# Retention unit by unit with 64-row matmuls, plain float32 scores and two PSUM banks

## The chip, the cores and the metric

One core of a Trainium2 chip runs the kernel. The metric is the device time of one execution in microseconds (us). Before the change the median of three runs is 960.05 us (959.32 to 961.3).

## The reference, cut to what matters

Three layers follow each other: a retention layer (linear attention with a decay per head) on 4 batches, 8 heads, 768 positions and head size 64; a feed-forward layer with an ELU on its 3072 tokens of 512 values; and a second one whose hidden 1024 values go through softmax-times-self and a layer norm.

```python
for t in range(S):
    state = gamma[None, :, None, None] * state + np.einsum('bhd,bhe->bhde', k[:, :, t], v[:, :, t])
    y[:, :, t] = scale * np.einsum('bhd,bhde->bhe', q[:, :, t], state)
...
x = np.ascontiguousarray(attn_out.transpose(0, 2, 1, 3)).reshape(B * S, H * D)
h = x @ w_in
g = np.where(h > 0.0, h, alpha * (np.exp(np.minimum(h, 0.0)) - 1.0))
return (g @ w_out).astype(np.float32)
```

## The kernel before, in words

**The retention.** Positions go in chunks of 128. A unit is four heads (two pairs) of one chunk; there are 48 units. For a pair the kernel needs: the scores k x q of each head, times a decay mask (line 187, or lines 201 to 203); the values, that is state x q (line 217) plus v x masked scores (line 219); the chunk's own k x v (line 223); the scaled result into `xf` (line 228); and the new state (lines 233 and 236). `xf` holds one block of 512 tokens.

The two heads of a pair share the 128 partitions, 64 each. Before the change the state is kept as a block diagonal 128 x 128 matrix per pair, so that one matmul serves both heads. The scores are made in two ways. For units 0 to 9 `kblk` holds k in a block diagonal with zeros and one plain float32 matmul per head runs over all 128 rows (line 186). For later units q and k are split into a high and a low part of the short float32 format (`split_unit`, on ScalarE and GpSimd), and one matmul of 256 columns per head gives two partial sums (line 199), which ScalarE and VectorE add up (lines 201 and 202).

**The feed-forward layers.** Every product of two float32 matrices is three matmuls of high and low parts (`mm3`, lines 65 to 67). Layer one runs over 6 blocks of 512 tokens, each in 16 steps s; a step makes one slice of the hidden layer (12 matmuls into `hp`, 128x512), its ELU, and 12 matmuls into the four `acc` banks, for the slice of two steps earlier. In block 0 the weights are prepared as well (`prep_w`: bits put together, clamped and split in high and low on VectorE, ScalarE and GpSimd). Layer two (from about 660 us) does 24 tiles of 128 tokens.

**The order.** The program's order is written out by hand, and every engine works its instructions off in that order; the SP queue issues all loads. First a prologue does units 0 to 7, which is the whole of block 0. Then each step does the matmuls into `hp`, then one pair of retention for the next block, then the matmuls into `acc`: pairs 18 to 95 lie in steps 0 to 77, one in each, and step 0 has pairs 16 and 17 as well. At a block's last step (k = 15) `xf` is split for the next block (`split_xh` on ScalarE, line 245, and `split_xl` on VectorE, line 250).

**PSUM.** `sc_bank` takes scores and `yu_bank` takes values and k x v; in the prologue three banks of each kind are used in turn, the others lent by `acc`.

## Time and profile before

| | |
|---|---|
| median of three runs | 960.05 us |
| the profiled execution | 957.76 us |
| its span, first to last instruction | 955.9 us |
| PE, matmuls busy | 928.9 us, 97% |
| VectorE (DVE) busy | 494.7 us, 52% |
| ScalarE (ACT) busy | 347.4 us, 36% |
| GpSimd (POOL) busy | 341.5 us, 36% |

The span is the time between the first and the last instruction of the profiled execution; 1.86 us of that execution lie around it. PE is the TensorE's matmuls, PEld its weight loads, which overlap them. Busy shares are means over stages with different limits: the stretch up to about 36 us is the prologue, that up to about 160 us is block 0 with its weight preparation, and the rest runs with prepared weights. Matmuls are pipelined, so that what a matmul costs is read from the start of one to the start of the next and not from its own length.

### The profile page before, as it was taken

The numbers are of one execution on the slowest core, as the hardware profiler recorded it, in microseconds if no ns is written. First come the engines' busy times: TensorE is split into PE (matmuls) and PEld (weight loads), VectorE is DVE, ScalarE is ACT, GpSimd is POOL, SyncE is SP. The second block draws the span as 40 slices with busy tenths as digits, with TensorE's granted clock in tenths as the row PEclk, the third lists the DMA queues.
The fourth block names the chain that finished last, engine by engine and source line by source line (L and its number), as shares of the span: only waits on it lengthen the run. The fifth ranks groups of instructions, "written<-read, shape, count | busy, mean of one in ns | idle before, by whom it ended". The sixth has DMA issues, their size and how long they took to land.

```text
span 955.9 us, 12630 instructions
## 1 busy us (share of the span) xinstructions
PE 928.9 (97%) x4776; PEld 760.0 (80%) x4776; DVE 494.7 (52%) x973; ACT 347.4 (36%) x629; POOL 341.5 (36%) x343
## 2 busy tenths in 40 slices
PE   6899999999999999999999999999999999999998
PEld 5677777888788887878788887888788888888886
DVE  3899997333443345333534328898633333333332
ACT  1355554333333334333332324443333333333332
POOL 2333232444534444444443423444322222222220
PEclk9999999999999999999999999999999999999999
DMA  8655551421142212322232214330211111111101
GB/s 253 195 177 179 182 171 39 121 78 53 64 121 78 77 48 78 113 78 77 70 91 77 80 67 138 95 91 20 77 45 45 45 45 44 45 45 45 45 23 44
DMA packets 43836, 82.67 MB, mean 86 GB/s; under 512 B 4096, under 2 KB 21120, under 8 KB 43776
## 3 DMA queue, kind: packets, MB, share of 16 engines
q1 hardware_dynamic: 43776, 81.88, 27.3%
q8 instruction: 37, 0.61, 0.3%
q14 instruction: 23, 0.19, 0.1%
HBM read 69.28 MB, written 12.58 MB: 86 GB/s over the span
## 4 chain that ended last, share of the span: by engine, by line
PE 79%; DVE 13%; DMA 2%; issue 2%; ACT 2%; SPq 1%; POOL 0%; ACTq 0%; DVEq 0%
PE hp L66 11%; PE hp L67 11%; PE hp L65 11%; PE acc L66 7%; PE acc L67 7%; PE acc L65 7%; PE op L66 5%; PE op L65 5%; PE op L67 5%; PE sc_bank L199 3%; PE yu_bank L219 2%; DVE wt L107 2%; PE tp L374 2%; DVE wt L108 2%; DVE xl L250 1%
## 5 line engine op out<-in xcount | busy, mean ns | idle before, releaser
L290 POOL TENSOR_TENSOR gl<-e,gh 128x512 fp32r<-128x512 f32 x80 | 108.1, 1351 | 249.2 <-ACT gh L282 201.7
L67 PE MATMUL acc<-gh,w1ol 128*128 128x512 f32 x384 | 150.7, 392 | 3.5 <-DVE w1ol L125 3.5
L67 PE MATMUL hp<-xh,w1il 128*128 128x512 f32 x384 | 150.4, 392 | 1.2 <-DVE w1il L125 1.2
L65 PE MATMUL acc<-gh,w1oh 128*128 128x512 f32 x384 | 151.2, 394 | 0.0
L66 PE MATMUL hp<-xl,w1ih 128*128 128x512 f32 x384 | 149.8, 390 | 1.1 <-DVE xl L250 0.9
L65 PE MATMUL hp<-xh,w1ih 128*128 128x512 f32 x384 | 149.9, 390 | 0.7 <-ACT xh L245 0.7
L66 PE MATMUL acc<-gl,w1oh 128*128 128x512 f32 x384 | 150.0, 391 | 0.0
L282 ACT CAST gh<-e 128x512 fp32r<-128x512 f32 x96 | 59.7, 622 | 199.7 <-DVE e L281 148.5
L271 ACT ACTIVATE e<-hp 128x512 f32<-128x512 f32 x80 | 47.8, 598 | 148.2 <-PE hp L67 147.3
L67 PEld LDWEIGHTS acc<-gh,w1ol 128*128 128x128 f32 x384 | 72.1, 188 | 21.2 <-DVE w1ol L125 6.3
L202 DVE TENSOR_TENSOR pt<-sa,sc_bank 128x256 f32<-128x256 f32 x60 | 25.3, 421 | 122.8 <-ACT sa L201 121.9
L67 PEld LDWEIGHTS hp<-xh,w1il 128*128 128x128 f32 x384 | 72.1, 188 | 18.9 <-DVE w1il L125 4.4
L66 PEld LDWEIGHTS hp<-xl,w1ih 128*128 128x128 f32 x384 | 72.1, 188 | 17.4 <-DVE xl L250 1.9
L65 PEld LDWEIGHTS hp<-xh,w1ih 128*128 128x128 f32 x384 | 72.1, 188 | 15.8 <-ACT xh L245 1.1
L65 PEld LDWEIGHTS acc<-gh,w1oh 128*128 128x128 f32 x384 | 72.2, 188 | 13.3 <-issue 0.5
L66 PEld LDWEIGHTS acc<-gl,w1oh 128*128 128x128 f32 x384 | 72.1, 188 | 12.8
L65 PE MATMUL op<-w2oh,zh 128*128 128x512 f32 x192 | 76.7, 399 | 0.0
L228 DVE TENSOR_TENSOR xf<-yu_bank,od_sb 128x256 f32<-128x256 f32 x43 | 18.1, 421 | 110.0 <-PE yu_bank L223 88.1
L66 PE MATMUL op<-w2ol,zh 128*128 128x512 f32 x192 | 74.8, 390 | 0.0
L67 PE MATMUL op<-w2oh,zl 128*128 128x512 f32 x192 | 74.8, 390 | 0.0
L67 PE MATMUL hp<-w2ih,yl 128*128 128x512 f32 x192 | 74.8, 389 | 0.0
L65 PE MATMUL hp<-w2ih,yh 128*128 128x512 f32 x192 | 74.8, 389 | 0.0
(101 smaller groups left out, 1573.1 us busy)
## 6 DMA issues: line engine op xcount, KB each, us to landing
in<-in_qkv SPq DMA_DIRECT2D x48, 384.0 KB, 4.4
qk<-in_qk_dup SPq DMA_DIRECT2D x30, 512.0 KB, 3.6
raw<-in_w_in SPq DMA_DIRECT2D x24, 512.0 KB, 4.3
raw<-in_w_out SPq DMA_DIRECT2D x24, 512.0 KB, 3.7
y_dr<-yt SPq DMA_DIRECT2D x24, 256.0 KB, 3.2
yin<-y_dr SPq DMA_DIRECT2D x24, 256.0 KB, 2.8
out<-ot SPq DMA_DIRECT2D x24, 256.0 KB, 2.0
kblk<-in_k_t SPq DMA_DIRECT2D x36, 64.0 KB, 4.5
```

The source lines that it names most:

```text
L65: nc.tensor.matmul(o, lh, rh, start=first, stop=False)
L66: nc.tensor.matmul(o, lh, rl, start=False, stop=False)
L67: nc.tensor.matmul(o, ll, rh, start=False, stop=last)
L107: nc.vector.scalar_tensor_tensor(b, t[:, :, 1], 0xC0000000, b, ALU.bitwise_and, ALU.bitwise_or)
L108: nc.vector.scalar_tensor_tensor(b, t[:, :, 0], 29, b, ALU.logical_shift_right, ALU.bitwise_or)
L199: nc.tensor.matmul(sc[:, j].rearrange("p a t -> p (a t)"), k2[:, 2 * i + j, :], q2[:, 2 * i + j].rearrange("p a t -> p (a t)"), start=True ...
L202: nc.vector.tensor_tensor(pt, sa, sc[:, :, 0, :], ALU.add)
L219: nc.tensor.matmul(yu[j * D:(j + 1) * D, i, 0, :], v[:, j * D:(j + 1) * D], pt[:, j, :], start=(c == 0), stop=True)
L271: nc.scalar.activation(e, h_t[s], AF.Exp)
L282: nc.scalar.copy(gh, e)
L290: engine.tensor_tensor(gl, e, gh.bitcast(F32), ALU.subtract)
L374: nc.tensor.transpose(tp[:, m, :], z[:, n, m * P:(m + 1) * P], ident)
```

## The change

The retention goes by units instead of pairs, and its tiles of the array change shape. `att_scores` multiplies k and q of one head on 64 rows (one half of the partitions), in plain float32 and with no zeros; heads j = 0 and j = 1 of a pair use the two row halves and write two banks. The state is no longer a block diagonal: it is 128 x 64 per pair, and `att_values` multiplies it in quarters, with row half j and column half i xor j, so that the four heads of a unit use the four quarters of the array. Rows of `xf` are permuted by that, and the host permutes the rows of the first weight matrix to match. Everything of a unit (values, k x v, scores) lies in the two banks of `ab`. `kblk`, `k_t`, `qk_dup`, `split_unit` and the sum of partial scores are gone; q, both forms of k, and v come in one load per unit, of the same bytes as before in units 0 to 9. The state's decay is read from a small table (`gm_sb`), so that one instruction serves both halves. In the steps a whole unit is done in each odd step, and none in the even ones, but for step 0.

```diff
--- before.py
+++ after.py
...
+    dm_sb = const.tile([P, 2, 2, 2 * P], F32, name="dm_sb")
     od_sb = const.tile([P, NP, P], F32, name="od_sb")
...
-        yu_bank = psa.tile([P, 512], F32, name="yu_bank")
+        ab = psa.tile([P, 2, 512], F32, name="ab")
         wb_p = ph1.enter_context(tc.tile_pool(name="wb", bufs=32))
...
@@ -145,95 +142,68 @@
         order2 = [("w2i", j) for j in range(2 * KD)] + [("w2o", j) for j in range(NF2)]
-        qk_t, in_t, hl_t, p_t = {}, {}, {}, {}
+        in_t, p_t = {}, {}
         def load_unit(u):
-            t = at_p.tile([P, 768], F32, tag="in", name="in", bufs=4)
+            t = at_p.tile([P, 4, 2 * P], F32, tag="in", name="in", bufs=4)
             nc.sync.dma_start(out=t, in_=qkv[u])
             in_t[u] = t
-            if u < UN:
-                for j in range(2):
-                    nc.sync.dma_start(out=kblk[u % 2][j * D:(j + 1) * D, :, j, :], in_=k_t[u, j * D:(j + 1) * D])
-        def load_qk(u):
-            t = hl_p.tile([P, 2, 4, P], F32, tag="qk", name="qk", bufs=1)
-            nc.sync.dma_start(out=t, in_=qk_dup[u - UN])
-            qk_t[u] = t
         def scale_k(u):
-            kt = in_t[u][:, 256:512].rearrange("p (h d) -> p h d", h=4)
+            kt = in_t[u][:, 2].rearrange("p (h d) -> p h d", h=4)
             h = 4 * (u % 2)
             nc.gpsimd.tensor_tensor(kt, kt, kd_sb[:, h:h + 4].unsqueeze(2).to_broadcast([P, 4, D]), ALU.mult)
-        def split_unit(u):
-            t = qk_t.pop(u)
-            q2 = hl_p.tile([P, 4, 2, P], F32R, tag="q2", name="q2")
-            k2 = hl_p.tile([P, 4, P], F32R, tag="k2", name="k2")
-            nc.scalar.copy(k2, t[:, 1])
-            nc.scalar.copy(q2[:, :, 0, :], t[:, 0])
-            nc.gpsimd.tensor_tensor(k2[D:], t[D:, 1], k2.bitcast(F32)[D:], ALU.subtract)
-            nc.gpsimd.tensor_tensor(q2[:, :, 1, :], t[:, 0], q2.bitcast(F32)[:, :, 0, :], ALU.subtract)
-            hl_t[u] = (q2, k2)
-        def att_scores_u(u, bank):
-            h = 4 * (u % 2)
-            pt = at_p.tile([P, 4, P], F32, tag="pt", name="pt")
-            sc = bank.rearrange("p (h t) -> p h t", h=4)
+        def att_scores(u, banks):
+            t = in_t[u]
             for i in range(2):
                 for j in range(2):
-                    nc.tensor.matmul(sc[:, 2 * i + j, :], kblk[u % 2][:, i, j, :], in_t[u][:, i * P:(i + 1) * P], start=True, stop=True)
-            nc.vector.tensor_tensor(pt, sc, dm_sb[:, h:h + 4, :], ALU.mult)
-            for i in range(2):
-                p_t[2 * u + i] = pt[:, 2 * i:2 * i + 2, :]
-        def att_scores(n, bank):
-            u, i = divmod(n, 2)
-            h = 4 * (u % 2) + 2 * i
-            pt = at_p.tile([P, 2, P], F32, tag="pt", name="pt")
-            q2, k2 = hl_t[u]
-            sc = bank.rearrange("p (j a t) -> p j a t", j=2, a=2)
-            for j in range(2):
-                nc.tensor.matmul(sc[:, j].rearrange("p a t -> p (a t)"), k2[:, 2 * i + j, :], q2[:, 2 * i + j].rearrange("p a t -> p (a t)"), start=True, stop=True)
-            sa = hl_p.tile([P, 2, P], F32, tag="sa", name="sa")
-            nc.scalar.copy(sa, sc[:, :, 1, :])
-            nc.vector.tensor_tensor(pt, sa, sc[:, :, 0, :], ALU.add)
-            nc.vector.tensor_tensor(pt, pt, dm_sb[:, h:h + 2, :], ALU.mult)
-            if i:
-                del hl_t[u]
-            p_t[n] = pt
-        def att_values(n, bank):
-            u, i = divmod(n, 2)
+                    r = slice(j * D, (j + 1) * D)
+                    c = slice(i * P, (i + 1) * P)
+                    nc.tensor.matmul(banks[j][:, 2 * P + i * P:2 * P + (i + 1) * P], t[r, 1, c], t[r, 0, c], start=True, stop=True)
+        def att_mask(u, views):
+            pt = at_p.tile([P, 2, 2 * P], F32, tag="pt", name="pt")
+            for j, v in views:
+                nc.vector.tensor_tensor(pt[:, j], v[:, :, 2 * P:], dm_sb[:, u % 2, j], ALU.mult)
+            p_t[u] = pt
+        def att_values(u, banks):
             c = u // 2 % NCH
             t = in_t[u]
-            yu = bank.rearrange("p (i a t) -> p i a t", i=2, a=2)
-            pt = p_t.pop(n)
-            p = 2 * (u % 2) + i
-            k, v = t[:, 256 + i * P:256 + (i + 1) * P], t[:, 512 + i * P:512 + (i + 1) * P]
+            pt = p_t.pop(u)
+            p0 = 2 * (u % 2)
+            half = lambda j: slice(j * D, (j + 1) * D)
+            out = lambda i, j: banks[j][half(i ^ j), :P]
+            heads = [(i, j) for i in range(2) for j in range(2)]
+            col = lambda i, j: slice((2 * i + j) * D, (2 * i + j + 1) * D)
             if c > 0:
-                nc.tensor.matmul(yu[:, i, 0, :], state[:, p, :], t[:, i * P:(i + 1) * P], start=True, stop=False)
-            for j in range(2):
-                nc.tensor.matmul(yu[j * D:(j + 1) * D, i, 0, :], v[:, j * D:(j + 1) * D], pt[:, j, :], start=(c == 0), stop=True)
+                for i, j in heads:
+                    nc.tensor.matmul(out(i, j), state[half(j), p0 + i, :], t[half(j), 0, i * P:(i + 1) * P], start=True, stop=False)
+            for i, j in heads:
+                nc.tensor.matmul(out(i, j), t[:, 3, col(i, j)], pt[:, j, i * P:(i + 1) * P], start=(c == 0), stop=True)
             if c < NCH - 1:
-                for j in range(2):
-                    r = slice(j * D, (j + 1) * D)
-                    nc.tensor.matmul(yu[r, i, 1, :D], k[:, r], v[:, r], start=True, stop=True)
-            if i == 0:
-                return
+                for i, j in heads:
+                    nc.tensor.matmul(banks[0][half(j), P + i * D:P + (i + 1) * D], t[:, 2, col(i, j)], t[:, 3, col(i, j)], start=True, stop=True)
+        def att_done(u, views):
+            c = u // 2 % NCH
             ci = u // 2 % CPB
             p0 = 2 * (u % 2)
-            nc.vector.tensor_tensor(xf[:, p0:p0 + 2, ci * P:(ci + 1) * P], yu[:, :, 0, :], od_sb[:, p0:p0 + 2, :], ALU.mult)
-            if c < NCH - 1:
-                for j in range(2):
-                    r = slice(j * D, (j + 1) * D)
-                    if c == 0:
-                        nc.vector.tensor_copy(state[r, p0:p0 + 2, r], yu[r, :, 1, :D])
-                    else:
-                        for p in range(p0, p0 + 2):
-                            nc.vector.scalar_tensor_tensor(state[r, p, r], state[r, p, r], GAMMA[2 * p + j] ** P, yu[r, p - p0, 1, :D], ALU.mult, ALU.add)
+            for j, v in views:
+                m = slice(p0, p0 + 2) if j == slice(0, 2) else slice(p0 + j.start, p0 + j.stop)
+                nc.vector.tensor_tensor(xf[:, m, ci * P:(ci + 1) * P], v[:, :, :P], od_sb[:, m, :], ALU.mult)
+            kv = views[0][1][:, 0, P:2 * P].rearrange("p (i d) -> p i d", i=2)
+            if c == 0:
+                nc.vector.tensor_copy(state[:, p0:p0 + 2, :], kv)
+            elif c < NCH - 1:
+                for i in range(2):
+                    s = state[:, p0 + i, :]
+                    nc.vector.scalar_tensor_tensor(s, s, gm_sb[:, p0 + i:p0 + i + 1], kv[:, i], ALU.mult, ALU.add)
             del in_t[u]
         x_t = {}
...
-        nc.vector.memset(state, 0.0)
-        for kb in kblk:
-            for j in range(2):
-                nc.gpsimd.memset(kb[j * D:(j + 1) * D, :, 1 - j, :], 0.0)
         nc.gpsimd.memset(half_n, -0.5)
...
         new_acc(0)
-        sc_banks = [sc_bank, *acc_t[0][:2]]
-        yu_banks = [yu_bank, *acc_t[0][2:]]
-        att_scores_u(0, sc_banks[0])
+        both = ([ab[:, 0], ab[:, 1]], [(slice(0, 2), ab)])
+        apart = lambda x: (x, [(slice(j, j + 1), x[j].unsqueeze(1)) for j in range(2)])
+        sets = [both, apart(acc_t[0][:2]), apart(acc_t[0][2:])]
+        att_scores(0, sets[0][0])
+        att_mask(0, sets[0][1])
         load_unit(2)
         scale_k(0)
         slot = -1
         XLE = (nc.vector, nc.gpsimd)
-        UB = PPB // 2
-        for u in range(UB):
-            if u + 1 < UB:
-                att_scores_u(u + 1, sc_banks[(u + 1) % 3])
-            if u + 3 < UB + 2:
+        for u in range(UPB):
+            if u + 1 < UPB:
+                att_scores(u + 1, sets[(u + 1) % 3][0])
+                att_mask(u + 1, sets[(u + 1) % 3][1])
+            if u + 3 < UPB + 2:
                 load_unit(u + 3)
             if u < 2:
                 load_w(order1[u])
             scale_k(u + 1)
-            for i in range(2):
-                att_values(2 * u + i, yu_banks[u % 3])
-            if u >= UB - 2:
+            att_values(u, sets[u % 3][0])
+            if u == UPB - 1:
+                att_scores(UPB, both[0])
+                att_mask(UPB, both[1])
+            att_done(u, sets[u % 3][1])
+            if u >= UPB - 2:
                 cs = range(2 * (u % 2), 2 * (u % 2) + 2)
                 split_xh(0, cs)
                 split_xl(0, cs, XLE)
-            if u == UB - 1:
-                att_scores_u(UB, sc_bank)
             if u in PRE:
                 prep_w(order1, slot)
...
         for s in range(NS + LAG):
             tb, k = divmod(s, NF1)
-            n = PPB + LEAD + s
-            u = n // 2
+            u = UPB + AHEAD + s // 2 if s % 2 else (UPB if s == 0 else NU)
...
-            if s == 0:
-                for m in range(PPB, PPB + LEAD):
-                    att_values(m, yu_bank)
-                load_unit(UB + 2)
-                att_scores_u(UB + 1, sc_bank)
-                scale_k(UB + 1)
-            if n < NPR:
-                att_values(n, yu_bank)
-            if n + 1 < NPR:
-                if (n + 1) // 2 >= UN:
-                    att_scores(n + 1, sc_bank)
-                elif n % 2 == 1:
-                    att_scores_u((n + 1) // 2, sc_bank)
+            if u < NU:
+                att_values(u, both[0])
+                if u + 1 < NU:
+                    att_scores(u + 1, both[0])
+                    att_mask(u + 1, both[1])
+                att_done(u, both[1])
+                if u + 2 < NU:
+                    load_unit(u + 2)
+                    scale_k(u + 1)
...
-                hl_p = ph0.enter_context(tc.tile_pool(name="hl", bufs=2, side="right", reuse_waits="tile"))
-                yt_p = hl_p
-                load_qk(UN)
-            if n % 2 == 1 and UN <= u + 2 < NU:
-                split_unit(u + 2)
-                if u + 3 < NU:
-                    load_qk(u + 3)
-            if n % 2 == 0 and u + 1 < NU:
-                scale_k(u + 1)
-            if n % 2 == 1:
-                if u + 2 < NU:
-                    load_unit(u + 2)
...
```

On TensorE, two successive steps after the weight preparation, before the change (the `acc` and `hp` matmuls between are cut to one row each; `in` holds q, k and v of a unit, `q` and `k` the split parts, `pt` the masked scores):

```order
L217 MATMUL yu_bank<-in,state 128x128
L219 MATMUL yu_bank<-pt,in 64x128 x2
L223 MATMUL yu_bank<-in 64x64 x2
L199 MATMUL sc_bank<-q_2309,k_2310 128x256 x2
L65 MATMUL acc<-gh,w1oh 128x512
...
L65 MATMUL hp<-xh,w1ih 128x512
...
L217 MATMUL yu_bank<-in,state 128x128
L219 MATMUL yu_bank<-pt,in 64x128 x2
L223 MATMUL yu_bank<-in 64x64 x2
L199 MATMUL sc_bank<-q_2423,k_2424 128x256 x2
```

and the same with the change, in one odd step:

```order
L186 MATMUL ab<-in,state 64x128 x4
L188 MATMUL ab<-pt,in 64x128 x4
L191 MATMUL ab<-in 64x64 x4
L167 MATMUL ab<-in 128x128 x4
L64 MATMUL acc<-gh,w1oh 128x512
```

A row's shape is that of its output. The two groups of ten become one of sixteen matmuls, with four in place of two instructions for the state's part, and all stand in one step.

On VectorE at the end of a block, where `xl` is made, before the change:

```order
L250 TENSOR_TENSOR xl<-xf,xh 128x512 x4
L228 TENSOR_TENSOR xf<-yu_bank,od_sb 128x2x128
L233 COPY state<-yu_bank 64x2x64 x2
L202 TENSOR_TENSOR pt<-sa,sc_bank 128x256
L203 TENSOR_TENSOR pt<-pt,dm_sb 128x256
L202 TENSOR_TENSOR pt<-sa,sc_bank 128x256
L203 TENSOR_TENSOR pt<-pt,dm_sb 128x256
```

and with it:

```order
L220 TENSOR_TENSOR xl<-xf,xh 128x512 x4
L172 TENSOR_TENSOR pt<-ab,dm_sb 128x512
L199 TENSOR_TENSOR xf<-ab,od_sb 128x2x128
L202 COPY state<-ab 128x128
L250 TENSOR_SCALAR e<-e 128x512
L251 TENSOR_TENSOR e<-e,hp 128x512
```

The first masked scores behind `xl` (`pt`) were for the very next step's values; now they are for the values two steps later, and one instruction makes them.

On the SP queue in the prologue, before the change:

```order
L152 DMA in<-in_qkv 128x768
L156 DMA kblk_112<-in_k_t 64x2x128 x2
L95 DMA raw<-in_w_in 128x1024
L152 DMA in<-in_qkv 128x768
L156 DMA kblk_111<-in_k_t 64x2x128 x2
L95 DMA raw<-in_w_in 128x1024
```

and with it:

```order
L152 DMA in<-in_qkv 128x1024
L92 DMA raw<-in_w_in 128x1024
L152 DMA in<-in_qkv 128x1024
L92 DMA raw<-in_w_in 128x1024
L152 DMA in<-in_qkv 128x1024
```

The two loads of `kblk` behind each load of a unit are gone, and that load is a third larger.

## Rows read from the trace of the kernel before

**Rows 1.** The page: busy time by engine, and the last chain's shares.

```profile
PE 928.9 (97%) x4776; PEld 760.0 (80%) x4776; DVE 494.7 (52%) x973; ACT 347.4 (36%) x629; POOL 341.5 (36%) x343
...
PE 79%; DVE 13%; DMA 2%; issue 2%; ACT 2%; SPq 1%; POOL 0%; ACTq 0%; DVEq 0%
```

**Rows 2.** Windows: length, busy PE, PEld, DVE, ACT, POOL, clock share, DMA share, GB/s.

```profile
60.00:100.00 40.00, 38.32 (x195) 29.23 (x194) 39.20 (x65) 22.09 (x40) 12.44 (x14) 1.00 0.56 178
100.00:160.00 60.00, 56.83 (x302) 44.28 (x303) 56.54 (x99) 32.10 (x58) 18.03 (x20) 1.00 0.44 135
160.00:320.00 160.00, 158.10 (x847) 129.40 (x846) 62.93 (x152) 54.51 (x104) 70.11 (x61) 1.00 0.26 84
```

**Rows 3.** Timeline, one step's retention on PE: start, length, instruction.

```profile
202.00 0.38 PE L217 MATMUL yu_bank<-in,state 128*128 128x128 f32 x2
...
202.31 0.44 PE L219 MATMUL yu_bank<-pt,in 128*64 128x128 f32 x4
...
202.58 0.28 PE L223 MATMUL yu_bank<-in 128*64 128x64 f32 x4
202.79 0.50 PE L199 MATMUL sc_bank<-q,k 128*128 128x256 f32 x2
...
203.14 0.39 PE L65 MATMUL acc<-gh,w1oh 128*128 128x512 f32 x1
```

**Rows 4.** Timeline, two places where tiles of the array change shape.

```profile
16.14 1.16 PE L186 MATMUL sc_bank<-in,kblk 128*128 128x128 f32 x8
17.14 0.39 PE L217 MATMUL acc<-in,state 128*128 128x128 f32 x2
...
52.85 0.44 PE L219 MATMUL yu_bank<-pt,in 128*64 128x128 f32 x4
...
53.22 0.50 PE L65 MATMUL acc<-gh,w1oh 128*128 128x512 f32 x1
...
53.55 0.40 PE L66 MATMUL acc<-gl,w1oh 128*128 128x512 f32 x1
```

**Rows 5.** Chain in block 0: two masks, one unit apart: start, length.

```profile
108.45 0.69 DVE pt L187
...
123.23 0.69 DVE pt L187
```

**Rows 6.** VectorE groups by line, 43 to 160 us: busy, mean ns, idle before.

```profile
L236 DVE SCALAR_TENSOR_TENSOR state<-state,yu_bank 64x64 f32<-64x64 f32 x16 | 2.8, 213 | 0.1
...
L233 DVE COPY state<-yu_bank 64x128 f32<-64x128 f32 x4 | 1.1, 284 | 0.0
```

**Rows 7.** Waits on PE: total us, times, longest.

```profile
PE sc_bank L186 <- DMA kblk<-in_k_t: 5.3, 2, 4.6
PE yu_bank L219 <- DVE pt L203: 4.5, 3, 1.9
PE acc L186 <- DMA kblk<-in_k_t: 4.0, 5, 1.1
```

**Rows 8.** Timeline of VectorE at the end of block 3.

```profile
468.51 3.60 DVE L250 TENSOR_TENSOR xl<-xf,xh 128x512 fp32r<-128x512 f32 x4
...
473.56 1.32 DVE L203 TENSOR_TENSOR pt<-pt,dm_sb 128x256 f32<-128x256 f32 x1
```

**Rows 9.** Waits of the SP queue in the prologue, 0 to 36 us.

```profile
SPq L156 <- PE acc L186: 6.8, 5, 2.2
SPq L156 <- PE sc_bank L186: 1.9, 3, 1.2
```

**Rows 10.** Windows of the prologue, columns as in rows 2.

```profile
0.00:4.00 4.00, 0.00 (x0) 0.00 (x0) 0.48 (x1) 1.28 (x1) 1.52 (x9) 1.00 0.46 126
12.00:16.00 4.00, 3.14 (x24) 2.95 (x24) 1.39 (x4) 0.00 (x0) 1.23 (x2) 1.00 0.90 280
28.00:32.00 4.00, 3.31 (x38) 2.82 (x34) 3.82 (x11) 0.68 (x1) 1.23 (x2) 1.00 1.05 307
```

**Rows 11.** Timeline of PE: the scores of unit 7.

```profile
29.94 1.13 PE L186 MATMUL acc<-in,kblk 128*128 128x128 f32 x8 [0.69 <-DMA kblk<-in_k_t]
```

More of the change, by code (lines that the diff above doesn't have):

```diff
@@ L32 @@
 NU = B * NCH * 2
-PPB = CPB * NP
+UPB = CPB * NP // 2
 LAG = 2
@@ L36, with tile_retention_ffn @@
 PRE = (2, 3, 4, 5)
-LEAD = 2
-UN = PPB + LEAD // 2 + 1
+AHEAD = 1
 E_MIN, E_MAX = (float(x) for x in np.array([896 << 20, 1151 << 20], np.uint32).view(np.float32))
-GAMMA = [1.0 - 2.0 ** (-5.0 - h) for h in range(H)]
 @with_exitstack
-def tile_retention_ffn(ctx, tc, k_t, qk_dup, qkv, w_in1, w_out1, w_in2, w_out2, g_ln, dmask, odec, kdec, ident_in, out):
+def tile_retention_ffn(ctx, tc, qkv, w_in1, w_out1, w_in2, w_out2, g_ln, dmask, odec, kdec, gdec, ident_in, out):
     nc = tc.nc
@@ L50, in tile_retention_ffn @@
     wa_p = ctx.enter_context(tc.tile_pool(name="wa", bufs=32))
-    dm_sb = const.tile([P, H, P], F32, name="dm_sb")
+    dm_sb = const.tile([P, 2, 2, 2 * P], F32, name="dm_sb")
     od_sb = const.tile([P, NP, P], F32, name="od_sb")
@@ L57, in tile_retention_ffn @@
     half_n = const.tile([P, 1], F32, name="half_n")
-    state = const.tile([P, NP, P], F32, name="state")
+    gm_sb = const.tile([P, NP], F32, name="gm_sb")
+    state = const.tile([P, NP, D], F32, name="state")
     xf = const.tile([P, KD, TB], F32, name="xf")
@@ L74, in tile_retention_ffn @@
         psa = pha.enter_context(tc.tile_pool(name="psa", bufs=1, space=PSUM, side="right"))
-        sc_bank = psa.tile([P, 512], F32, name="sc_bank")
-        yu_bank = psa.tile([P, 512], F32, name="yu_bank")
+        ab = psa.tile([P, 2, 512], F32, name="ab")
         wb_p = ph1.enter_context(tc.tile_pool(name="wb", bufs=32))
@@ L84, in tile_retention_ffn @@
         stage_p = ph0.enter_context(tc.tile_pool(name="stage", bufs=4, side="right"))
-        kblk = [at_p.tile([P, 2, 2, P], F32, name=f"kblk{i}", bufs=1) for i in range(2)]
         raw_t, abs_t, w1i, w1o, w2i, w2o = {}, {}, {}, {}, {}, {}
@@ L482, in tile_retention_ffn @@
                 ph0 = ExitStack()
-                hl_p = ph0.enter_context(tc.tile_pool(name="hl", bufs=2, side="right", reuse_waits="tile"))
-                yt_p = hl_p
-                load_qk(UN)
-            if n % 2 == 1 and UN <= u + 2 < NU:
-                split_unit(u + 2)
-                if u + 3 < NU:
-                    load_qk(u + 3)
-            if n % 2 == 0 and u + 1 < NU:
-                scale_k(u + 1)
-            if n % 2 == 1:
-                if u + 2 < NU:
-                    load_unit(u + 2)
-            if n == NPR - 1:
+                yt_p = ph0.enter_context(tc.tile_pool(name="yt0", bufs=3, side="right", reuse_waits="tile"))
+            if u == NU - 1:
                 ph0.close()
@@ L579, in _layouts @@
         "g_ln": moe2_g_ln.reshape(NF2, P).T,
-        "dmask": dmask.astype(np.float32),
+        "dmask": dmask[:, hd.transpose(0, 2, 1)].reshape(P, 2, 2, 2 * P).astype(np.float32),
         "odec": odec.reshape(P, NP, P).astype(np.float32),
         "kdec": kdec.astype(np.float32),
+        "gdec": gdec.astype(np.float32),
         "ident": np.eye(P, dtype=np.float32),
```

19 lines of the change are left out of this document (9 added, 10 removed).

## The prediction

> **What bounds the kernel now.** I read the page's busy times and chain first: PE is busy 97% of the span, and 79% of the chain that ended last is PE's, 13% VectorE's [rows 1]. So a saving on PE counts wherever PE is what ends last. The windows tell where that is. From 160 us on PE is busy 158 of 160 us and VectorE 63: PE's own pace. From 60 to 100 us VectorE is busy 39.2 of 40 us [rows 2]: VectorE's pace, and PE waits a little in every step. Two units' masks in that stretch lie 14.8 us apart [rows 5]; that is the time of two steps. Then the waits on PE: small, and of two kinds that this change touches, `kblk` loads in the prologue and masked scores (L203) at block ends [rows 7]. The granted clock is 1.00 in all windows, the 2.4 GHz level, so no term hangs on it.
>
> **The prices on PE.** A matmul's price is the distance from its start to the next one's. In rows 3 and 4 I take a step apart. Eight plain float32 passes of 128 columns (a float32 matmul is two instructions) and one first weight load take 1.00 us from 16.14 to 17.14 [rows 4]; with 0.11 for the load that is 0.11 a pass. L217 to L219 is 0.31 us: two passes of 0.107 and 0.10 that is left over, where the array's tile goes from 128 columns to 64 [rows 3]. L219 to L223, no change of tile, is 0.27 for four passes of two heads: if they ran one behind the other it would be 0.43 and more, so the two column halves run side by side: 0.05 for a first weight load and two times 0.107. L223 to L199 is 0.21: four half-length passes in two pairs of 0.053, and 0.10 for the change of tile. L199 to L65 is 0.35: 0.11 of exposed weight load and two times 0.12. The same load shows as 0.33 from L65 to L66 right behind a change of tile, where 512 columns usually take about twice the 0.12 of L199's 256 [rows 4]. So a change of tile costs 0.10 us of draining and then the first weight load, 0.05 us (64 columns) or 0.11 us (128 columns): 0.15 or 0.21 us together.
>
> **A unit in the steps from s = 17 on.** Before: two pairs of 1.14 us, from 202.00 to 203.14 [rows 3], 2.28 us. After, by these prices:
> - change to quarters 0.15, and state x q: four quarters side by side, two passes, 0.21;
> - change to 128 rows x 64 columns 0.15, and the values: eight passes in four pairs, 0.43;
> - k x v, same tile: four pairs of half length, 0.21;
> - change to 64 rows x 128 columns 0.21, and the scores: eight passes in four pairs, 0.45;
> - change back to the full array 0.21.
>
> Sum 2.02 us, so 0.26 us saved. The changes of tile are four before and four after; what shrinks is the stream. The split scores cost 4 x 0.12 = 0.48 per unit, the plain ones 0.45: no gain there. State x q goes from 4 x 0.107 to 2 x 0.107. The rest is two separate first loads less. The four units without a state save 0.19 by the same count; over the 31 units from unit 17 to 47 I take 0.25 each: **-7.7 us**.
>
> What no row shows is two row halves side by side, and four quarters. Bounds: full overlap as the column halves have it [rows 3], or none between row halves. Without it the state takes 0.43 (the column halves still overlap) and the scores 0.90. I take full overlap, since the nearest row, that of the column halves, shows the array running independent tiles; the other end is a rival below. The two new tile shapes' changes could cost less than 0.15, down to nothing, if only the columns matter: up to 2 x 0.15 x 31 = 9.3 us more gain. I take the measured one. The Trainium skill ("TensorE: Matmul & The Clock Gate", Part 3, measured speedup) gives 3.07x for four row tiles in place of 4x. No run here shows it; by it, as an estimate, state and scores together (0.66) would take 0.86, and the sum would come 6 us higher.
>
> ScalarE's and GpSimd's splits and VectorE's additions of partial scores go too. That is worth nothing: from 160 us on none of the three is busy for half of the time (63, 54.5 and 70 of 160 us) [rows 2]. Masks and results now wait for a whole unit, but what they make is asked for two steps later.
>
> **Block ends.** Behind the last step of a block VectorE makes `xl` for 3.60 us, from 468.51, and only then the masked scores, done at 474.9 [rows 8], which the next step's L219 waits for: three times, 4.5 us in all [rows 7]. After the change no retention lies in that next step, so nothing asks. What is late next is `xl` for the next `hp`; it was ready in time before, and the unit now in the step ahead gives it 0.9 us more. **-4.5 us**, between 0 and that.
>
> **Block 0 (43 to 160 us).** PE's saving is lost here; the time is VectorE's. Its instructions go from four state updates to two and from two copies to one. An update takes 0.21 us, a copy 0.28 [rows 6]; columns are as many as before (the copy's twice as many in 128 partitions but once), the decay comes from a table instead of a constant. Five of the nine units update (2 x 0.21 less, some of it overlapped: 0.36), two copy (0.28): 5 x 0.36 + 2 x 0.28 = 2.4, of which I take **-2.0 us**; bounds 0 (the new forms take twice the time) and -2.7. VectorE hardly waits before these (0.1 us in all [rows 6]), so that both behind a unit's scores costs it nothing.
>
> **The prologue.** Loads set its pace: PE waits for `kblk`, 5.3 and 4.0 us [rows 7], of which the first 4.6 is the first load and stays. The SP queue, from which all loads come in order, stands 6.8 + 1.9 us waiting for PE to free `kblk` [rows 9], and what is queued behind it (weights, the next units) waits too. The loads move 280 to 307 GB/s at a DMA share of 0.90 to 1.05 [rows 10], so without these stalls they can gain only a little rate. Up to unit 7's load the queue has 8 units and 4 weights of 512 KB and 768 KB of constants, 7.08 MB; 0.50 MB are there at 4 us, and the rest takes 21.4 to 23.5 us at these rates. Unit 7's scores could then start at 25.4 to 27.5 in place of 29.94 [rows 11]: 2.4 to 4.5 us. The scores and mask of unit 8 now stand ahead of the block's last results on VectorE, and their load comes two loads (1.05 MB, 3.5 us) after unit 7's, about when those results are due. I take **-3.3 us**; bounds -4.7 (all the later waits go) and +1 (unit 8's load is late).
>
> **Sum.** -7.7 - 4.5 - 2.0 - 3.3 = -17.5 us. The profiled execution is 957.76 us, so 940.3; the median of the runs stands 2.3 us above it, and I forecast 960.05 - 17.5 = 942.5 us. Its own range is 937 to 949.
>
> **Rivals.**
> - *Row halves take turns.* The two row halves share the columns of the array and its way out to PSUM; the column halves that overlap in rows 3 share neither. If they run one after the other, 27 units with a state lose 0.21 and all 31 lose 0.45: 19.7 us, **962 us**. Slower than before begins where a unit loses more than 17.5 / 31 = 0.56 us. If each turn from one row half to the other also costs a change of tile, 0.15 three times in the state and 0.21 three times in the scores, with the column overlap gone too, a unit loses 2.2 us: about **1005 us**. Nothing in the profile excludes it; the tiles in rows 3 speak for independence. Chance 0.08 and 0.03.
> - *Passes keep the program's order.* A head's two passes use the same tile and stand together in the program; if no later head may overtake, only one head's second pass runs beside the next head's first. State then takes five passes (+0.32), scores five (+0.11): 27 x 0.32 + 31 x 0.11 = 12, **955 us**. The Trainium skill says so ("TensorE: Matmul & The Clock Gate", Part 3, the mechanism: matmuls start and end strictly in program order). The trace disagrees for column halves: L219 would take 0.05 + 3 x 0.107 = 0.37 and takes 0.27. Chance 0.05.
> - *Prologue and block 0 stay as they are.* VectorE is busy 3.82 of 4 us from 28 us on [rows 10], so faster loads may only uncover it, and its saving in block 0 is a few short instructions: 942.5 + 5.3 = **948 us**. Chance 0.16.
> - *Only a change of columns drains.* **933 us**, chance 0.08; nothing speaks for it but that rows 3 and 4 show no other kind of change.
>
> **Chances.** Forecast 0.60; with the rivals the sum is 1. A difference under 0.2% (1.9 us) could not be told from none here. Faster: 0.60 + 0.16 + 0.08 + 0.05 = 0.89. The turns at 962 lie on the border: half to the same, 0.04, and half with the 1005 to slower, 0.07. The range 933 to 957 leaves out the turns and the tails.
>
> **What would show it.** In a step of the later blocks: 16 matmuls from the first quarter to the first `acc` within about 2.0 us; the starts of four quarters, and of two scores, a few ns apart. Wrong if the scores' eight passes take 0.9 us, or if the quarters start 0.1 us apart. No wait for masked scores behind block ends. Masks in block 0 some 14.4 us apart where they were 14.8, VectorE still full. No wait of the SP queue for PE at unit loads but for a free buffer, and unit 7's scores at 25 to 28 us. Even steps without retention hold 24 matmuls and nothing else.

## The result and the profile after

The changed kernel takes 944.33 us (median of 4 runs, 943.30 to 945.35), the kernel before in the same comparison 959.94 us (959.32 to 961.30): ratio 0.9835, interval 0.9818 to 0.9852, 1.65% faster. Forecast were 942.5 us. The profiled executions are 944.98 and 957.76 us, spans 943.2 and 955.9: on the traces, from which every term is read, the gain is 12.7 us and not 17.5. The two executions differ in TensorE's mean granted clock, 0.999 before and 0.994 after; what that makes of the gain stands at the end of the account of the prediction.

The page of the kernel after: busy time, and shares of the last chain, as in [rows 1].

```profile
PE 915.7 (97%) x5056; PEld 736.5 (78%) x5056; DVE 450.7 (48%) x820; ACT 293.9 (31%) x509; POOL 262.0 (28%) x278
...
PE 84%; DVE 11%; issue 2%; DMA 2%; ACT 1%; POOL 0%; SPq 0%; ACTq 0%
```

Two windows of after, columns as in [rows 2]:

```profile
60.00:100.00 40.00, 36.84 (x188) 27.90 (x189) 39.23 (x64) 23.32 (x42) 12.84 (x14) 1.00 0.55 189
...
160.00:320.00 160.00, 160.00 (x959) 128.69 (x960) 49.76 (x104) 33.75 (x57) 39.62 (x37) 1.00 0.19 60
```

PE's share of the chain rose from 79 to 84%, and in the window from 160 to 320 us PE has no gap at all. One unit's retention in a step of after (start, length, instruction), which answers to [rows 3, 4]:

```profile
197.19 0.39 PE L66 MATMUL hp<-xh,w1il 128*128 128x512 f32 x1
197.51 0.45 PE L186 MATMUL ab<-in,state 64*64 64x128 f32 x8
197.89 0.66 PE L188 MATMUL ab<-pt,in 128*64 128x128 f32 x8
198.38 0.40 PE L191 MATMUL ab<-in 128*64 128x64 f32 x8
198.71 0.71 PE L167 MATMUL ab<-in 64*128 64x128 f32 x8
199.35 0.50 PE L64 MATMUL acc<-gh,w1oh 128*128 128x512 f32 x1
199.69 0.39 PE L65 MATMUL acc<-gl,w1oh 128*128 128x512 f32 x1
```

From 197.51 to 199.35 are 1.84 us; the step into it (0.32 us where two such matmuls are usually 0.23 apart) adds 0.09, the first full matmul behind it (0.34 for 0.23) about 0.14 with the next: 2.07 us a unit, where two pairs took 2.31 by the same count. In the trace's single records the four quarters' first passes start at 197.512, .519, .526 and .532, their second ones from 197.672 on; a pair of scores starts 6 ns apart, and the next pair 0.11 us later.

Where the 12.7 us lie is seen from the first matmul of the same tile in both timelines. The kernel before, at the first, third and nineteenth step, late in layer one, and in layer two:

```profile
36.09 0.48 PE L65 MATMUL hp<-xh,w1ih 128*128 128x512 f32 x1
...
49.70 0.47 PE L65 MATMUL hp<-xh,w1ih 128*128 128x512 f32 x1
...
166.28 0.39 PE L65 MATMUL hp<-xh,w1ih 128*128 128x512 f32 x1
...
574.47 0.39 PE L65 MATMUL hp<-xh,w1ih 128*128 128x512 f32 x1
...
740.12 0.39 PE L65 MATMUL hp<-w2ih,yh 128*128 128x512 f32 x1
```

The kernel after, the same five:

```profile
31.78 0.79 PE L64 MATMUL hp<-xh,w1ih 128*128 128x512 f32 x1
...
48.83 0.50 PE L64 MATMUL hp<-xh,w1ih 128*128 128x512 f32 x1
...
163.35 0.39 PE L64 MATMUL hp<-xh,w1ih 128*128 128x512 f32 x1
...
559.26 0.39 PE L64 MATMUL hp<-xh,w1ih 128*128 128x512 f32 x1
...
724.64 0.39 PE L64 MATMUL hp<-w2ih,yh 128*128 128x512 f32 x1
```

After is ahead by 4.3 us at the first step, by 0.9 at the third, 2.9 at the nineteenth, 15.2 late in layer one, 15.5 in layer two, and 12.7 at the end. So the later steps gave all that was forecast (12.3), most of the prologue's gain was lost within two steps, and layer two, which the change does not touch, lost 2.8 us again from its eighth tile, shown here, to the end.

The waits on PE in after (total, times, longest), against [rows 7]:

```profile
PE acc L66 <- DVE w1ol L122: 6.4, 7, 1.1
...
PE hp L66 <- DVE w1il L122: 3.1, 1, 3.1
```

The masked scores at block ends are no longer among them. At the end of a block VectorE still makes `xl` first, as in [rows 8], but what follows nobody asks for yet:

```profile
455.96 3.59 DVE L220 TENSOR_TENSOR xl<-xf,xh 128x512 fp32r<-128x512 f32 x4
459.47 0.68 DVE L172 TENSOR_TENSOR pt<-ab,dm_sb 128x512 f32<-128x512 f32 x1
```

The second step of after on PE. The last brackets are idle time and what ended it:

```profile
37.96 0.50 PE L64 MATMUL hp<-xh,w1ih 128*128 128x512 f32 x1
...
41.84 0.79 PE L66 MATMUL hp<-xh,w1il 128*128 128x512 f32 x1 [3.15 <-DVE w1il L122]
42.43 0.63 PE L64 MATMUL hp<-xh,w1ih 128*128 128x512 f32 x1
42.86 0.63 PE L65 MATMUL hp<-xl,w1ih 128*128 128x512 f32 x1
```

And VectorE, which PE waits for there:

```profile
33.46 0.69 DVE L220 TENSOR_TENSOR xl<-xf,xh 128x512 fp32r<-128x512 f32 x1
37.99 0.69 DVE L172 TENSOR_TENSOR pt<-ab,dm_sb 128x512 f32<-128x512 f32 x1 [3.84 <-PE ab L167]
...
41.10 0.68 DVE L122 TENSOR_TENSOR w1il<-wt,w1ih 128x512 fp32r<-128x512 f32 x1
```

VectorE has nothing to do for 3.84 us, since the mask of unit 9 stands ahead of the weight's low part in its program and PE reaches unit 9's scores only behind the first step. Then it comes to `w1il` 3 us too late. The clock pays as well. Windows of after, three of the prologue, against [rows 10], and one of the second step (the clock is the third number from the end):

```profile
24.00:28.00 4.00, 1.98 (x32) 1.51 (x32) 3.93 (x9) 0.00 (x0) 1.43 (x2) 1.00 0.88 326
28.00:32.00 4.00, 2.89 (x33) 2.29 (x34) 2.90 (x9) 1.14 (x2) 1.04 (x1) 0.83 0.97 353
32.00:36.00 4.00, 4.00 (x12) 2.66 (x12) 2.05 (x6) 1.14 (x2) 2.66 (x4) 0.74 0.06 25
...
40.90:47.70 6.80, 5.86 (x24) 4.11 (x26) 4.82 (x8) 2.89 (x6) 2.02 (x2) 0.50 0.68 231
```

PE was busy 1.98 of 4 us (24 to 28), then the granted clock fell to 0.83 and 0.74 in the first step. It fell again towards the end of the wait for `w1il`, to 0.50 from 40.90 to 47.70, the 1.2 GHz level: full matmuls stand 0.43 us apart there (42.43 to 42.86) where they usually stand 0.23.

What the second fall costs is seen in the trace of a kernel that is the same up to layer two (32 unused bytes on the other side, below). Its second step has the same wait and no fall:

```profile
40.34 0.50 PE L66 MATMUL hp<-xh,w1il 128*128 128x512 f32 x1 [3.15 <-DVE w1il L122]
...
44.72 0.50 PE L64 MATMUL hp<-xh,w1ih 128*128 128x512 f32 x1
```

```profile
36.46:44.72 8.26, 5.11 (x45) 3.58 (x45) 7.66 (x14) 3.94 (x8) 2.61 (x3) 1.00 0.48 159
```

From the first matmul of that step to the first of the next are 8.26 us and not 10.87, so the lower level alone made 2.6 us. Three traces of this order of work with 3.4 us of that level in the step lie between, at 9.74 to 9.81. Of the eight traces with this wait of 3.1 to 3.2 us seven have the fall in the step, of the six without the wait none.

The loads themselves gained: 326 to 353 GB/s here, and unit 7's scores start at 24.16, against 29.94 in [rows 11].

### The profile page after: what moved, and what is told of

Read it like the earlier page. It is cut to its first block, busy times and chain, and to the rows that moved or that the text cites. A ratio compares the mean times of both kernels' runs of the same rounds, so it can differ in the third digit from the quotient of the medians.

```text
span 943.2 us, 12562 instructions
## 1 busy us (share of the span) xinstructions
PE 915.7 (97%) x5056; PEld 736.5 (78%) x5056; DVE 450.7 (48%) x820; ACT 293.9 (31%) x509; POOL 262.0 (28%) x278
## 4 chain that ended last, share of the span: by engine, by line
PE 84%; DVE 11%; issue 2%; DMA 2%; ACT 1%; POOL 0%; SPq 0%; ACTq 0%
PE hp L65 12%; PE hp L66 12%; PE hp L64 12%; PE acc L64 8%; PE acc L66 8%; PE acc L65 8%; PE op L66 5%; PE op L65 5%; PE op L64 5%; PE ab L167 2%; PE ab L188 2%; DVE wt L104 2%; PE tp L344 2%; DMA in<-in_qkv 2%; DVE wt L105 1%
## 5 line engine op out<-in xcount | busy, mean ns | idle before, releaser
L64 PE MATMUL acc<-gh,w1oh 128*128 128x512 f32 x384 | 154.0, 401 | 0.0
L172 DVE TENSOR_TENSOR pt<-ab,dm_sb 128x512 f32<-128x512 f32 x43 | 29.6, 688 | 158.7 <-PE ab L167 158.7
L250 DVE TENSOR_SCALAR e<-e 128x512 f32<-128x512 f32 x80 | 34.8, 435 | 135.8 <-ACT e L241 135.7
L65 PE MATMUL hp<-w2il,yh 128*128 128x512 f32 x192 | 75.8, 395 | 0.0
```

What stands on the lines that cost most here:

```text
L64: nc.tensor.matmul(o, lh, rh, start=first, stop=False)
L65: nc.tensor.matmul(o, lh, rl, start=False, stop=False)
L172: nc.vector.tensor_tensor(pt[:, j], v[:, :, 2 * P:], dm_sb[:, u % 2, j], ALU.mult)
L250: nc.vector.tensor_scalar(e, e, 1.0, -1.0, ALU.min, ALU.add)
```

## The experiments

**Row halves and order of passes.** The first kernel takes the overlap of row halves away: scores and state x q of all heads read the lower row half (so the upper heads compute on other heads' data).

```
-                    r = slice(j * D, (j + 1) * D)
+                    r = slice(0, D)
...
-                    nc.tensor.matmul(out(i, j), state[half(j), p0 + i, :], t[half(j), 0, ...
+                    nc.tensor.matmul(out(i, j), state[half(0), p0 + i, :], t[half(0), 0, ...
```

> The changed kernel, but scores and state x q of all heads read the lower row half (head j = 1 gets j = 0's operands; the output is not the reference's). So the two row halves can't run side by side, with all else equal. Theory of the prediction (the halves overlap fully): in the later blocks the scores' eight passes go from 0.65 to 1.10 us from their first start to the first acc matmul, state x q from 0.38 to 0.59, so a unit costs 0.66 more, and 31 units with 27 states 19.7 us: about 964 us. Rival (row halves take turns already): no change, 944 us.

Measured 975.36 us (one run). A unit in the steps, on PE:

```profile
289.73 0.65 PE L186 MATMUL ab<-in,state 64*64 64x128 f32 x8
290.31 0.66 PE L188 MATMUL ab<-pt,in 128*64 128x128 f32 x8
...
291.13 1.16 PE L167 MATMUL ab<-in 64*128 64x128 f32 x8
292.21 0.50 PE L64 MATMUL acc<-gh,w1oh 128*128 128x512 f32 x1
```

State x q takes 0.58 us (0.38 in the changed kernel), the scores 1.08 (0.64): 2.49 for 1.84, 0.65 more, as worked out. From the nineteenth step on it loses 19.5 us, so the overlap of row halves is real and worth that here. The other 10.9 us were lost before that step, which I had not expected (about 964 us): up to 45 us TensorE goes at half pace, with the 128-column passes 0.21 us apart and not 0.11 (more on that at the end).

The second writes the heads in another order, both pairs of the lower row half first.

```
-            for i in range(2):
-                for j in range(2):
+            for j in range(2):
+                for i in range(2):
...
-            heads = [(i, j) for i in range(2) for j in range(2)]
+            heads = [(i, j) for j in range(2) for i in range(2)]
```

> The changed kernel with the heads of a unit written in another order: both pairs of the lower row half, then both of the upper, in the scores, and in the state, value and kv matmuls the two heads j=0 before the two heads j=1. The same instructions on the same tiles. If each part of the array works off its own queue and only the parts' own order counts: scores pairs no longer start 6 ns apart at the head of the queue, but once all eight passes are issued the four of a row half still run beside the four of the other if the sequencer runs ahead of the array: unit in the steps 1.84 us as now, run 944 to 946. If the array takes instructions in program order and only overlaps neighbours: the scores lose their overlap almost wholly (+0.43 us a unit) and the quarters half of theirs, the unit is 2.2 to 2.4 us, and the run is 960 to 975 with the prologue.

Measured 947.09 us (one run), a unit 1.90 us. The quarters still start together, and the scores of the upper half start 13 ns behind those of the lower, though four passes of the lower stand ahead of them in the program:

```profile
325.87 0.45 PE L186 MATMUL ab<-in,state 64*64 64x128 f32 x8
...
327.12 0.72 PE L167 MATMUL ab<-in 64*128 64x128 f32 x8
```

So independent tiles of the array do overtake each other, over four instructions here; the other order costs 0.06 us a unit, not the 0.4 and more of the rival. The Trainium skill ("TensorE: Matmul & The Clock Gate", Part 3, the mechanism) has matmuls start and end strictly in program order; in this trace, first passes of later heads start before second passes of earlier ones, so the measurement decides against it for separate tiles. A record does not name its head; that passes a few ns apart belong to different tiles follows from the 0.107 us that one pass takes on its tile.

**The prologue.** One more column of the first weights is prepared in the prologue, behind unit 7, where VectorE idled.

```
-PRE = (2, 3, 4, 5)
+PRE = (2, 3, 4, 5, 7)
```

> The changed kernel with one more column of the first weights prepared in the prologue, behind unit 7 (PRE gets a 7). Theory: the prologue's gain of 4.3 us was given back because hp(1) then waited for w1il (3.15 us at 41.84), VectorE having idled 3.84 us before; the added preparation fills that idle time, so hp(1) does not wait: s2 starts 2.5 to 4 us earlier than the 48.83 of the changed kernel, and the run is 940.5 to 942 against 944.3. Rival: the preparation delays VectorE's masks for units 8 and 9 and PE is at its slower level (0.43 us a matmul) either way, so s2 stays at 48.8 within 0.7 and the run within 1 us of 944.3.

Measured 939.50 us, a little under the 940.5 to 942 expected, ratio 0.9784 (0.9755 to 0.9814). Its starts, as above, of the first, second, third and nineteenth step:

```profile
31.34 0.50 PE L64 MATMUL hp<-xh,w1ih 128*128 128x512 f32 x1
...
37.45 0.50 PE L64 MATMUL hp<-xh,w1ih 128*128 128x512 f32 x1
...
42.31 0.47 PE L64 MATMUL hp<-xh,w1ih 128*128 128x512 f32 x1
...
157.04 0.39 PE L64 MATMUL hp<-xh,w1ih 128*128 128x512 f32 x1
```

The second step now takes 4.86 us and not 10.87; its wait and the slow matmuls are gone (granted clock 1.00 in every window from 20 to 60 us). At the third step the kernel is 6.5 us ahead of the changed one, more than expected, and at the nineteenth 6.3. Some 2.6 us of that are the lower level in the changed kernel's one trace; the medians differ by 4.8.

The same line in the kernel before tells whether that is the change's gain or would have come anyway.

> The kernel before, with one more weight preparation behind unit 7 of its prologue. Theory that the changed kernel lost its prologue gain again because VectorE had run dry where PE was early: before the change PE comes to hp(1) at 43.7, 5.7 us later, VectorE is not late there, and the added preparation only delays unit 7's and 8's masks: 958 to 961 us, ratio 0.998 to 1.002. Rival: a column more in the prologue relieves block 0 whatever PE does: 953 to 956, as much as the 4.8 us that it gave the changed kernel.

Measured 955.80 us (11 runs, 952.99 to 962.62), ratio 0.9954 (0.9931 to 0.9976): the rival's number, my theory's is outside. In its trace the nineteenth step starts at 164.26, 2.0 us earlier than before, and late in layer one 0.4 us are left. Of these 2.0 us 1.5 go in one step: PE waits 1.8 us for masked scores at the end of a block, right behind that the granted clock falls (0.65 in the window from 260 to 264 us, 0.92 in the next), and matmuls of that step start up to 0.43 us apart. In the trace of the kernel before the same wait brings no fall. With this preparation in both, the change is ahead by 5.5 us at the first step (36.83 and 31.34), 7.0 at the third (49.31 and 42.31) and 7.2 at the nineteenth. So in this pair of traces, neither of which shows a fall of the clock up to there, nothing of the prologue's gain is given back. In the medians the change gives 16.3 us with the preparation in both and 15.6 without it, which the spread of the runs does not tell apart. Where the other part of the 3.7 us lies that the preparation gives the kernel before in the median, I cannot place.

Whether the clock alone made the first two steps slow is tested by an idle matmul behind each of the units 3 to 7:

```
+            if 3 <= u < UPB:
+                fill = psh.tile([P, 512], F32, tag="h", name="fill")
+                nc.tensor.matmul(fill, dm_sb[:, 0, 0, :P], dm_sb[:, 0].rearrange(...), start=True, stop=True)
```

> The changed kernel with one idle plain float32 matmul of 512 columns on known data into a free bank after each of the units 3 to 7 of the prologue, so that TensorE is busier between 20 and 31 us. Theory: hp(0) ran at 0.43 us a matmul because TensorE had been busy under half of the time before it (1.98 of 4 us in 24:28); with the fill the granted clock of 28:36 stays at 1.00, hp(0)'s 12 matmuls take 2.7 to 3.3 us and not 6.2, and s1 starts 1 to 2 us earlier than 37.96; the end moves only if hp(1)'s wait for w1il (VectorE) does not take it back, so the run is 942.5 to 944.5. Rival: the level falls for a reason that TensorE's load doesn't change: s0 and s1 where they are or 0.5 to 2 us later by the fill's own 0.9 us each, run 944.3 to 946.

Measured 945.41 us, ratio 0.9841 (0.9809 to 0.9873), in the rival's range and not the theory's. The windows with the fill, and then a matmul of its first step:

```profile
28.00:32.00 4.00, 3.53 (x36) 2.04 (x35) 2.37 (x7) 1.14 (x2) 1.45 (x2) 1.00 0.93 348
32.00:36.00 4.00, 3.54 (x12) 1.93 (x12) 2.16 (x6) 1.14 (x2) 2.22 (x3) 1.00 0.05 18
```

```profile
34.36 0.50 PE L65 MATMUL hp<-xl,w1ih 128*128 128x512 f32 x1 [0.22 <-DVE xl L220]
```

The granted clock stays at 1.00 there and matmuls that wait for nothing run 0.23 us apart, yet the first step ends where it did, since it waits for `xl` instead. So in the first step the level cost nothing. The second step is not tested by this: its wait for `w1il` (3.1 us) stayed, the granted clock fell as in the changed kernel (0.60 in the window from 40 to 44 us, 0.55 in the next), and the third step starts at 48.83 in both.

**Layer two.** Nothing of the change runs there, but the 24 first matmuls of a tile take 5.60 us where they took 5.45. What moved is where things lie: the state is 1024 bytes a partition smaller, the decay table takes 32, so what stands behind them moved by 992 bytes. I tried other offsets: 32 unused bytes on that side (960 off), 32 on the other side, in a small pool of its own (960 between the two as well), the kernel before with 32 bytes less, the changed kernel with 992 (0 off) and 480 bytes (512 off).

```
     gm_sb = const.tile([P, NP], F32, name="gm_sb")
+    pad = const.tile([P, 248], F32, name="pad")      # or 120 words; the 8 words stand behind `state`
     state = const.tile([P, NP, D], F32, name="state")
```

```
-            rs = sm_p.tile([P, 1], F32, tag="rs", name="rs")
+            rs = sm_p.tile([P, 1], F32, tag="rs", name="rs", bufs=3)   # kernel before
```

> The changed kernel with 32 unused bytes per partition behind its constants, so that all weights and activations on that side of SBUF lie 32 bytes higher. In the changed kernel layer two's 576 matmuls into hp start 233.5 ns apart (before the change 226.7), which makes 3.9 us. Theory A: what slows them is that their streamed operand (w2i) now begins at a multiple of 64 bytes and their weights (yh, yl) at 32 beyond one; before, both lay 32 beyond. With the pad both lie 32 beyond again: 226.7 ns, and 3.9 us faster than the changed kernel, about 940.4 us. Theory B: the clock or a neighbour in time (mean clock 0.994) slows them: 233.5 ns stay, and 944 us.

> The changed kernel with 32 unused bytes ahead of yh and yl instead, on the other side of SBUF, so that yh and yl begin at multiples of 64 bytes, as w2i does. Theory A (the two operands differ in their place within 64 bytes): 226.7 ns, about 940.4 us. Theory A2 (a streamed operand at a multiple of 64 bytes is slow in itself): 233.5 ns stay, and 944 us. Theory B (clock or neighbours): 233.5 ns stay.

> The kernel before the change, with one small buffer fewer (rs, 3 in place of 4), so that all weights lie 32 bytes lower: w2i at multiples of 64 bytes, yh and yl 32 beyond. Nothing else differs. Theory A and A2: layer two's hp matmuls go from 226.7 to 233.5 ns, 3.9 us slower than before, about 963.8 us. Theory B: no change, 960 us.

> The changed kernel with 992 unused bytes a partition beside the state, so that everything that lay behind it in SBUF is where it was in the kernel before. Theory: the spacing of layer two's first matmuls depends on where the weights and the streamed tile lie to each other: 24 of them take 5.45 us as before (5.60 in the changed kernel, 5.50 with 32 bytes), which over 24 tiles is 3.6 us: run 940 to 941, the prologue unchanged (s2 at 48.8). Rival: the spacing also hangs on something else that the change moved (order or PSUM): it stays at 5.50 to 5.60, run 941 to 944.5.

> The changed kernel with 480 unused bytes a partition beside the state: what lies behind it in SBUF is then 512 bytes from where it was in the kernel before (992 in the changed kernel, 960 with the pad of 32, 0 with the pad of 992). Theory: what counts is the distance between weights and streamed tile within a unit of 512 bytes or less, so 512 is like 0: a tile's 24 first matmuls of layer two take 5.45 us, run 940 to 941. Rival: only a distance of 0 gives 5.45, any other multiple of 64 gives 5.50 as 960 did (run 941 to 942), and what is no multiple of 64 gives 5.60.

| kernel | offset, bytes | 24 matmuls, us | run, us | ratio (interval) |
|---|---|---|---|---|
| before | 0 | 5.45 | 959.94 | |
| after | 992 | 5.60 | 944.33 | 0.9835 (0.9818-0.9852) |
| after + 32 | 960 | 5.50 | 940.96 | 0.9805 (0.9762-0.9848) |
| after + 32, other side | 960 | 5.50 | 942.03 | 0.9809 (0.9769-0.9849) |
| before, 32 less | 32 | 5.59 | 963.09 | 1.0032 (1.0012-1.0052) |
| after + 992 | 0 | 5.45 | 940.10 | 0.9790 (0.9761-0.9818) |
| after + 480 | 512 | 5.45 | 943.43 | 0.9827 (0.9790-0.9864) |

The first of a tile's 24 matmuls in the changed kernel and what follows the last, and then the same two with the pad of 992 bytes:

```profile
724.64 0.39 PE L64 MATMUL hp<-w2ih,yh 128*128 128x512 f32 x1
...
730.24 0.92 PE L344 MATMUL tp<-ident,z 128*128 128x128 f32 x7
```

```profile
724.61 0.39 PE L65 MATMUL hp<-w2ih,yh 128*128 128x512 f32 x1
...
730.06 0.60 PE L345 MATMUL tp<-ident,z 128*128 128x128 f32 x4
```

These are 5.60 us there and 5.45 here; the granted clock is 1.00 in that tile of the changed kernel, so it is not the clock. The spacing goes with the offset, in the kernel before too, and not with which side moved. Five offsets give three prices: 0 and 512 the least, 960 a little more, 32 and 992 the most. Theory A, places within 64 bytes, gave the time of the kernel before with 32 bytes less (963.8 expected, 963.09 measured), but not the price of the two pads, which should have been that of offset 0. The run followed it where expected (3.6 us expected and 4.2 measured for 992), except with 480 bytes, where the tiles are at 5.45 and the run is only 0.9 us faster, 943.4 for the expected 940 to 941: there `op` takes 5.57 us a tile (5.54 with the pad of 992), 24 x 0.03 = 0.7, and the prologue was 0.5 us later; the rest is within the spread of the runs, and by its interval this run cannot be told from the changed kernel's.

**Both together.** The pad of 992 bytes with the preparation behind unit 7, and a further one behind unit 6:

```
-PRE = (2, 3, 4, 5)
+PRE = (2, 3, 4, 5, 7)          # second kernel: (2, 3, 4, 5, 6, 7)
...
+    pad = const.tile([P, 248], F32, name="pad")
```

> The changed kernel with both edits that helped by themselves: 992 unused bytes beside the state (24 tiles of layer two at 5.45 us, -3.6 us) and one more weight preparation behind unit 7 (s18 at 157.0 for 163.4, -6.3 us on the trace, -4.8 us on the medians). If they are independent, the run is 944.3 - 3.6 - 4.8 = 936 (934.5 to 937.5), ratio to the kernel before 0.975. Rival: the addresses also change how the prologue's loads and PE run, so that the prologue gives part of it back: 937.5 to 939.5.

> As the kernel with pad and one more preparation, and one more behind unit 6 as well. VectorE was busy 3.9 of 4 us between 20 and 28 already, so a preparation after unit 6 delays the masks of units 7 and 8 by its 2 to 3 us; what it saves is the same work later, in block 0, where VectorE sets the pace as well (14.3 us a pair of steps). Theory: VectorE's work is only moved: within 1 us of the kernel with one preparation (935 to 937). Rival: PE's wait in the prologue grows by the whole preparation: +2 to +3 us.

The first took 936.80 us, ratio 0.9761 (0.9735 to 0.9788), the fastest here and within its expectation. Together the edits give 7.5 us, alone 4.2 and 4.8, so they add up to within 1.5 us; the four runs spread over 2.9. The second took 939.95, ratio 0.9793 (0.9768 to 0.9818), 3.2 us more, a little over the rival's +2 to +3: its first step waits 3.6 us for `xh`, and behind that wait the granted clock is 0.51 (35 to 42 us); the second step starts at 42.19, with one preparation at 39.70.

## Why the prediction was right, and where not

- *Units in the later steps, and block ends.* Forecast -7.7 and -4.5, measured from the nineteenth step to late in layer one -12.3. A unit came to 2.07 us for 2.02, and before to 2.31 for 2.28: 0.24 saved for 0.25. The unknown, overlap of row halves and of quarters, was full, as the column halves in [rows 3] had it; taken away it costs 0.65 us a unit. A change of tile to a new shape cost what the old shapes' did, so the 933 us case is out. The 3.07x of the Trainium skill ("TensorE: Matmul & The Clock Gate", Part 3, measured speedup) would have made state and scores 0.2 us longer; in the rows of the unit they take 0.38 and 0.64 us with their changes of tile, for 0.36 and 0.66 in the sum.
- *Block 0.* Forecast -2.0, measured from the third to the nineteenth step 114.52 us for 116.58: -2.1. Masks of two units stand 14.30 us apart (106.25 and 120.55), forecast 14.4. One price in it was off: an update takes 0.27 us in its new form (64 columns, all partitions), not the 0.21 of [rows 6].
- *Prologue: the step that failed in the profiled execution.* "I take -3.3 us", with unit 7's scores at 25.4 to 27.5. The loads did better than that, 24.16, and the first step began 4.3 us early; but I let that gain run through to block 0, though [rows 10] showed VectorE busy 3.82 of 4 us there. It ran into a wait for `w1il` of 3.15 us, and 0.9 us were left at the third step. The wait is what the rival at 948 us said ("faster loads may only uncover it"). But 2.6 us of the loss are the 1.2 GHz level behind it, where the prediction had that no term hangs on the clock; in the trace with the wait and without that level the third step starts at 44.72, 5.0 us ahead of the kernel before (its first step began 5.8 us ahead, at 30.27). That the wait brings the level is likely by the count of traces above, and not shown. With VectorE's idle time used, both are gone. The bound of +1 us that I gave for this term held it.
- *Layer two: not in the sum.* 24 tiles at 0.15 us, 3.6 us, of which a shorter start of the layer hides a part. The changed price is shown by the offsets, the reason for it is not. I had looked at which instructions change, and not at what a smaller tile does to the addresses of those that don't.
- *The sum.* On the traces -12.7 for -17.5: -4.3 and not -3.3 in the prologue's loads, +3.4 lost at once, +2.8 in layer two. The time forecast is 1.8 us off and not 4.8 because the profiled run of before was 2.2 us under its median and that of after 0.65 over its own. For the sum that is luck, but it has a cause: the runs go with their mean granted clock. All runs of the kernel before at 1.00 took 956.24 to 957.71 us, those at 0.998 957.84 to 960.32, those at 0.994 960.75 to 963.13. Its profiled execution had 0.999, that of after 0.994; at 0.994 in both the change gives 15.8 to 18.2 us. So a part of what the traces lack to 17.5 is clock, which the sum did not have.

## What to carry to other kernels

Take small matmuls apart by the distance of their starts, one tile shape at a time: column halves told here what row halves and quarters would cost, to 0.05 us a unit. Where a stage is early, ask which engine stands in program order behind the new gap, and put work into it. Before two traces are subtracted, compare their granted clocks, stretch by stretch. And when a tile's size changes, look at the spacing of matmuls that the change doesn't touch.

## What the runs showed of the hardware

- Independent tiles of the array run fully side by side: four 64 x 64 quarters start 6 to 7 ns apart, two 64 x 128 halves 6 ns, 13 ns when four passes of the other half stand between them.
- The spacing of 128 x 512 matmuls is 226.7 ns, about 229 or 233.5 ns by where weights and streamed tile lie to each other (offsets above). Why, no run here shows.
- A granted clock of 1.00 at the start of a trace is no reading. Records of the granted clock begin at 13.61 us in the changed kernel's trace, at 15.89 in that of the kernel before and at 45.27 with the state and scores in one row half; windows ahead of them print 1.00, as the first of [rows 10] does. Up to there the pace is that of the 1.2 GHz level: with one row half, passes of 128 columns start 0.21 us apart, eight scores take 2.00 us in the prologue and 1.08 in the later steps (291.13 to 292.21), and full matmuls go over from 0.43 to 0.23 us apart right at the first record (below). PE had been busy without a gap since 8 us; why the level rose so late, no run here shows. The forecast's remark on the clock (1.00 in all windows) held for the later steps only.

```profile
44.71 0.63 PE L65 MATMUL hp<-xl,w1ih 128*128 128x512 f32 x1
45.14 0.46 PE L66 MATMUL hp<-xh,w1il 128*128 128x512 f32 x1
45.44 0.40 PE L64 MATMUL hp<-xh,w1ih 128*128 128x512 f32 x1
45.67 0.39 PE L65 MATMUL hp<-xl,w1ih 128*128 128x512 f32 x1
```
